# A fused sparse-attention and PReLU-MLP kernel: one token chunk taken off the seven-product scheme, one product split, one sum halved

## Chip, cores and metric

The kernel runs on one core of a Trainium2 chip. The metric is the device time of one execution in microseconds: 337.81 us before the change (median of three runs, 337.74 to 339.4).

## What is computed

Eight batches of eight heads, 576 positions, head size 64. Four heads use a local mask of 32 positions, four a strided mask. The attention output, laid out as 4608 tokens of 512 features, goes through a two-layer network whose activation is a PReLU with one slope per hidden feature:

```python
mask_local = (rel >= 0) & (rel < stride)                       # heads 0 to 3
mask_strided = (rel >= 0) & (pos[None, :] % stride == pos[:, None] % stride)   # heads 4 to 7
attn = softmax(where(mask, q @ k.T / 8, -1e9))
x = (attn @ v).transpose(0, 2, 1, 3).reshape(4608, 512)
h = x @ w_in                                                    # 512 -> 2048
g = np.maximum(h, 0.0) + alpha * np.minimum(h, 0.0)
out = g @ w_out                                                 # 2048 -> 512
```

## The kernel before

The network is done in nine chunks of 512 tokens, numbered 0 to 8. The attention of later batches is cut into small pieces that are laid between the steps of the network, so that TensorE (PE) is kept busy. The order of all instructions on each engine is the order in which the Python code emits them: each engine works off its own list in that order, and waits where an operand or a buffer isn't ready.

A chunk has two parts. **Layer 1** (`lin1_piece`) has 16 pieces. Each makes 128 of the 2048 hidden features for 512 tokens with four matmuls (line 637) into one of three PSUM banks hb0 to hb2, which `hbank` hands out in turn. ScalarE (ACT) takes the negative part (line 647), and VectorE (DVE) finishes the PReLU and writes it as f16 into gT (line 650, the "finish"). Only then is the bank free. The finish is put into the list `late`, which the next attention step empties.

**Layer 2** is done plainly in chunk 0: `lin2_piece`, 16 steps of four 512-column matmuls (line 664), and for each 128 tokens a copy by ACT (line 669) and a store. In chunks 1 to 8 `lin2_sums` computes the same product of a 512 x 2048 and a 2048 x 512 matrix as two by two blocks with seven products in place of eight. Each product has two halves (`mt` 0 and 1) of eight 256-column matmuls (line 759). It needs four sums of blocks of gT, called gsum 0 to 3 in the profile (g1, g2, g4, g3 in the code, line 706), each 128 x 2048 in f16, and four differences of blocks of w_out, made once (`w_sums`, line 694; the third, w3, overwrites a block of w_out). The index p in the code stands for these products:

- p 0 is P1, block (0,0) of gT with block (0,0) of w_out, bank A
- p 1 is P5, gsum 0, bank B; p 2 is P6, gsum 1, added on to bank A
- p 3 is P3, gsum 2, added on to bank B; p 4 is P7, gsum 3, added on to bank A, with w3
- p 5 is P2, block (0,1) of gT, bank C; p 6 is P4, block (1,1) of gT, added on to bank A

ACT copies the banks to SBUF after P1, P5 and P6 (k1, k5, k2, line 771). After P3, P7 and P2, DVE adds a bank and one of these copies into an output tile (line 774), which the sync queue stores. The fourth output tile is a copy by ACT after P4. Chunks 7 and 8 ("quiet", no attention is left) run the products in the order of p. Chunks 1 to 6 run P1, P2, P5, P6, P3, P7, P4.

Who makes the sums: in chunk 1 all four are on DVE, the one for P7 as two halves between layer-1 pieces (after pieces 10 and 12). In chunks 2 to 6 these two halves are on GpSimd (POOL), and the other three on DVE: two at the start of layer 2, the third at its step 4.

Attention works on pairs of heads, four pairs per batch. For batches 2 and up: `transpose_piece` turns q and k of the local heads with PE (line 252) into a PSUM tile from a pool of three banks ("ps"), and DVE copies q, ACT copies k to SBUF (lines 194 and 192); `tails` does the last 64 positions (line 282, the "tail transpose"). q and k of the strided heads are loaded by POOL's queue into qsd and ksd and turned by a transposing DMA on the sync queue (line 141). `score_both` makes scores (line 412), ACT takes the exponential (lines 425 and 431), POOL multiplies by the mask (lines 427 and 434). `pv_piece` multiplies by v (line 455), into the same three banks, and DVE divides by the row sum (lines 462 and 464). POOL also converts and rearranges loaded q, k and v (line 196) and issues many loads.

Of the kernel before, what the change touches and what calls it, by code (L numbers as in the profile page):

```python
# [9 lines left out]
F32 = mybir.dt.float32  # L10
# [21 lines left out]
def kernel(  # L32
# [10 lines left out]
    nc = tc.nc  # L43
    keep = tc.keep_in_program_order

    B, H, S, D = q.shape
# [8 lines left out]
    spool = ctx.enter_context(tc.tile_pool(name="stage", bufs=3))  # L55
# [5 lines left out]
    kpool = ctx.enter_context(tc.tile_pool(name="kp", bufs=1))  # L61
# [26 lines left out]
    turn, busy = [0, 1], []  # L88
# [101 lines left out]
    def cast_copy(eng, o, i):  # L190
        if eng == "act":
            keep(nc.scalar.copy(o, i))
        elif eng == "dve":
            keep(nc.vector.tensor_copy(o, i))  # L194
        else:
            keep(nc.gpsimd.tensor_copy(o, i))
# [41 lines left out]
    def transpose_piece(u, nm):  # L238

        b, strided = u // 2, u % 2 == 1
        early = b < NEARLY
        src = cast16[(b, strided, nm)]
        dst = qTs[u % 2][:, :, 0:576] if nm == "q" else kTs[u % 2][:, :, 32:608]
        tp = pspool.tile([128, 8, 64, 2], F16, tag="ps", name="tp")
        for j in range(8):
            blk = (src[:, j % 2, 128 * (j // 2) : 128 * (j // 2) + 128] if strided  # L250
                   else src[:, j].rearrange("p f d -> p (f d)"))
            keep(nc.tensor.transpose(tp[:, j].rearrange("r p e -> r (p e)"), blk, ident))  # L252
        if strided:
            main = tp.rearrange("r j p e -> r e j p")
            o = dst.rearrange("r e (j p) -> r e j p", j=8)[:, :, :, 0:64]
        else:
            main = tp.rearrange("r t p e -> r e p t")
            o = dst[:, :, 0:512].rearrange("r e (p t) -> r e p t", t=8)
        if early:
            for e in range(2):  # L260
                eng = "dve" if (nm == "q") == (e == 0) else "act"
                if u == 0 and nm == "q":
                    eng = "act"
                if nm == "k" and e == 1:
                    tails(b, u, strided)
# [277 lines left out]
    for g in range(7, npair + 2):  # L543
        c = g // 4
# [68 lines left out]
    late = []  # L613
# [82 lines left out]
    def g_sum(eng, n, which, k0, k1):  # L696

        g = gTs[n]
        g1, g2, g4, g3 = gsum
        o, x, y, op = {  # L700
            1: (g1, quad(g, 1, 0), quad(g, 1, 1), ALU.add),
            2: (g2, g1, quad(g, 0, 0), ALU.subtract),
            3: (g3, quad(g, 0, 0), quad(g, 1, 0), ALU.subtract),
            4: (g4, quad(g, 0, 1), g2, ALU.subtract),
        }[which]
        keep(eng.tensor_tensor(o[:, k0:k1], x[:, k0:k1], y[:, k0:k1], op=op))  # L706
# [10 lines left out]
    def quiet(n):  # L717

        return n >= NCH - 2

    def lin2_sums(n, i):

        g = gTs[n]
        last = n == NCH - 1
        p, mt = i // 2, i % 2
        if i == 0:
            tiles = [banks[z] for z in turn]
            lay.clear()
# [27 lines left out]
        dst = lay[bank][mt]  # L756
        own = mt == 0 or (last and bank == "A")
        for kf in range(8):
            keep(nc.tensor.matmul(  # L759
                dst, lhs[:, kf, 128 * mt : 128 * mt + 128], rhs[:, kf, :],  # L760
                start=(first and own and kf == 0), stop=(kf == 7), skip_group_check=True))

        def each(fn, o, *more):

            if last and bank == "A":
                fn(o[:, mt], lay["A"][mt], *[z[:, mt] for z in more])
            elif mt == 1:
                fn(o, lay[bank + "f"].rearrange("p (m c) -> p m c", m=2), *more)

        def act(o, x):  # L770
            keep(nc.scalar.copy(o, x))  # L771

        def add(o, x, y):
            keep(nc.vector.tensor_tensor(o, x, y, op=ALU.add))  # L774

        def new(nm):
            if mt == 0:
                pool, tag = (kpool, nm) if nm[0] == "k" else (opool, "osb")
                if nm == "k1":
                    pool, tag = (spool, "v") if quiet(n) else (kpool, "k2")  # L780
                held[nm] = pool.tile([128, 2, 256], F32, tag=tag, name=nm, **({"bufs": 2} if tag == "v" else {}))
            return held[nm]

        if p == 0:
            each(act, new("k1"))
        elif p == 1:
            each(act, new("k5"))
        elif p == 2:
            each(act, new("k2"))
        elif p == 3:  # L790
            each(add, new("o12"), held["k2"])
            if mt:
                store(n, 0, 1, held["o12"])
        elif p == 4:
            each(add, new("o22"), held["k5"])
            if mt:
                store(n, 1, 1, held["o22"])
        elif p == 5:
            each(add, new("o11"), held["k1"])
            if mt:  # L800
                store(n, 0, 0, held["o11"])
# [130 lines left out]
    for n in range(1, NCH):  # L932
        ab = attn_until(n + 1) if n + 1 < B else len(pieces)
        left = ab - pos["i"]
        skip = 4 if n == 1 else 0
        acc = 0.0
        for i in range(30):
            if i < 16:
                if quiet(n):
                    lin1_piece(n, 8 * (i % 2) + i // 2)  # L940
                    if i in (3, 7, 11):
                        late.append(lambda i=i: g_sum(nc.gpsimd, n, 1, i // 2 - 1, i // 2 + 1))
                else:
                    lin1_piece(n, i)
                    if i in (10, 12):
                        g_sum(nc.vector if n == 1 else nc.gpsimd, n, 3, 2 * i - 20, 2 * i - 16)
                if n == 1 and i == 6:
                    w_sums(nc.vector, (3,))
            else:
                lin2_sums(n, i - 16)  # L950
            if i >= skip:
# [38 lines left out]
```

The softmax here doesn't subtract the row's maximum and nothing guards it: scores larger than these inputs give would overflow.

## Time and profile before

The profiled execution took 345.34 us, 343.6 us from the first to the last instruction. That is longer than the timed runs.

| engine | busy us | share of the span | instructions |
|---|---|---|---|
| PE (matmul) | 310.0 | 90% | 2861 |
| DVE | 239.6 | 70% | 412 |
| ACT | 174.7 | 51% | 325 |
| POOL | 174.5 | 51% | 170 |

The chain of work that ended last is PE for 67% of the span, DVE for 18%, and ACT and DMA for 5% each. The chunks start at 33.3 us (chunk 0), 72.4, 120.0, 156.8, 190.2, 224.0, 257.2, 287.9 and 313.9.

How to read the lines that follow: a timeline line has the start, the duration, the engine, the source line, the operation, output<-input with shapes, the count, and in brackets the idle time in front of it and what ended that. A line of the table of waits has who waited for whom, then the total in us, the number of times and the longest. In the table by stretches "x" stands ahead of the number of instructions.

### The profile page before, as it was taken

The numbers are of one execution on the slowest core, as the hardware profiler recorded it, in microseconds if no ns is written. First come the engines' busy times: TensorE is split into PE (matmuls) and PEld (weight loads), VectorE is DVE, ScalarE is ACT, GpSimd is POOL, SyncE is SP. The second block draws the span as 40 slices with busy tenths as digits, with TensorE's granted clock in tenths as the row PEclk, the third lists the DMA queues.
The fourth block names the chain that finished last, engine by engine and source line by source line (L and its number), as shares of the span: only waits on it lengthen the run. The fifth ranks groups of instructions, "written<-read, shape, count | busy, mean of one in ns | idle before, by whom it ended". The sixth has DMA issues, their size and how long they took to land.

```text
span 343.6 us, 7176 instructions
## 1 busy us (share of the span) xinstructions
PE 310.0 (90%) x2861; PEld 203.4 (59%) x2861; DVE 239.6 (70%) x412; ACT 174.7 (51%) x325; POOL 174.5 (51%) x170
## 2 busy tenths in 40 slices
PE   6699999999377979899989998999899999999995
PEld 2355445544146734685477887855774586486484
DVE  4336774669998447965895589568847994874872
ACT  1345655547333556447735763577357615633640
POOL 8762595031946868466938690869071720300300
PEclk9659999999969989999999999999999999999999
DMA  7999999399209699169919990897171013003003
GB/s 228 179 207 208 247 165 153 70 166 264 40 19 124 112 236 139 20 133 258 126 18 138 273 117 23 124 171 91 32 156 50 19 38 106 0 2 123 0 2 122
DMA packets 81569, 40.38 MB, mean 118 GB/s; under 512 B 58480, under 2 KB 77184, under 8 KB 81536
## 3 DMA queue, kind: packets, MB, share of 16 engines
q0 software_dynamic: 41728, 17.38, 44.3%
q1 hardware_dynamic: 39808, 22.55, 28.4%
q8 instruction: 22, 0.36, 0.4%
q14 instruction: 11, 0.09, 0.1%
HBM read 38.01 MB, written 9.44 MB: 138 GB/s over the span
## 4 chain that ended last, share of the span: by engine, by line
PE 67%; DVE 18%; ACT 5%; DMA 5%; issue 2%; SPq 0%; ACTq 0%; DVEq 0%
PE hb L637 27%; PE hb L759 23%; DVE gsum L706 6%; DVE gT L650 5%; PE hb L664 4%; DMA kT<-ksd 3%; DMA kl<-in_k_dram 2%; PE pv L455 2%; PE hb L826 2%; DVE x L464 2%; DVE o L774 2%; PE tp L252 2%; ACT neg L647 2%; DVE qT L194 1%; PE sp L412 1%
## 5 line engine op out<-in xcount | busy, mean ns | idle before, releaser
L637 PE MATMUL hb<-xT,win 128*128 128x512 f16 (+1 forms) x640 | 135.4, 362 | 6.0 <-DVE gT L650 5.3
L650 DVE SCALAR_TENSOR_TENSOR gT<-neg,oma,hb 128x512 f16<-128x512 f32 x144 | 105.3, 743 | 43.8 <-ACT neg L647 36.9
L647 ACT ACTIVATE neg<-hb 128x512 f32<-128x512 f32 x144 | 86.0, 597 | 50.0 <-PE hb L637 49.7
L637 PEld LDWEIGHTS <-win 128*128 128x128 f16 x640 | 60.8, 98 | 63.5 <-issue 11.0
L427 POOL TENSOR_TENSOR et<-et,consts 128x576 f16<-128x576 f16 (+1 forms) x24 | 30.6, 1277 | 77.2 <-ACT et L425 77.1
L759 PEld LDWEIGHTS <-gsum 128*128 128x128 f16 x512 | 47.3, 98 | 6.7 <-DVE gsum L706 0.8
L706 POOL TENSOR_TENSOR gsum<-gT 128x1024 f16<-128x1024 f16 (+1 forms) x16 | 28.0, 1765 | 43.0 <-DVE gT L650 43.0
L759 PEld LDWEIGHTS <-gT 128*128 128x128 f16 x384 | 36.1, 98 | 9.5 <-issue 4.1
L464 DVE TENSOR_TENSOR x<-pv,rc 96x384 f16<-96x384 f32 (+2 forms) x62 | 33.0, 532 | 2.1
L434 POOL TENSOR_TENSOR et<-et,consts 128x576 f16<-128x576 f16 (+1 forms) x24 | 32.4, 1349 | 1.8 <-ACT et L431 0.9
L759 PE MATMUL hb<-wout,gT 128*128 128x256 f16 x248 | 31.8, 275 | 0.0
L462 DVE RECIPROCAL rc<-pv 72x6 f32<-72x6 f32 (+2 forms) x80 | 14.7, 183 | 24.1 <-PE pv L455 24.0
L455 PEld LDWEIGHTS <-et 72*128 72x128 f16 (+1 forms) x448 | 24.6, 99 | 11.5 <-POOL et L434 3.1
L759 PE MATMUL hb<-wsum,gsum 128*128 128x256 f16 x248 | 31.0, 273 | 0.0
L759 PE MATMUL hb<-wout,gsum 128*128 128x256 f16 x248 | 30.2, 273 | 0.7 <-DVE gsum L706 0.7
L771 ACT COPY k<-hb 128x512 f32<-128x512 f32 (+1 forms) x24 | 13.6, 568 | 31.7 <-PE hb L759 31.7
L774 DVE TENSOR_TENSOR o<-hb,k 128x512 f32<-128x512 f32 (+1 forms) x24 | 16.3, 680 | 16.9 <-PE hb L759 12.7
L425 ACT ACTIVATE et<-sp 128x576 f16<-128x576 f32 (+1 forms) x24 | 15.5, 647 | 15.0 <-PE sp L412 15.0
L706 DVE TENSOR_TENSOR gsum<-gT 128x2048 f16<-128x2048 f16 (+2 forms) x12 | 21.9, 1824 | 0.3
L826 PE MATMUL hb<-gsum 128*128 128x512 f16 x44 | 18.1, 486 | 1.2 <-DVE gsum L838 1.2
L431 ACT ACTIVATE et<-sph 128x288 f16<-128x288 f32 (+1 forms) x48 | 18.1, 410 | 1.9 <-PE sph L412 1.9
L184 POOL DMA_DIRECT2D vl<-in_v_dram x8 | 11.2, 1403 | 14.4 <-PE pv L455 13.3
(108 smaller groups left out, 340.2 us busy)
## 6 DMA issues: line engine op xcount, KB each, us to landing
out_dram<-o SPq DMA_DIRECT2D x31, 256.0 KB, 2.9
ql<-in_q_dram SPq DMA_DIRECT2D x6, 512.0 KB, 5.4
kl<-in_k_dram SPq DMA_DIRECT2D x6, 512.0 KB, 7.3
stv<-in_v_dram POOLq DMA_DIRECT2D x8, 288.0 KB, 7.4
vl<-in_v_dram POOLq DMA_DIRECT2D x6, 384.0 KB, 9.0
win<-in_moe_w_in_dram POOLq DMA_DIRECT2D x4, 512.0 KB, 9.1
wout<-in_moe_w_out_dram POOLq DMA_DIRECT2D x4, 512.0 KB, 13.5
qsd<-in_q_dram POOLq DMA_DIRECT2D x6, 288.0 KB, 7.1
```

Source lines behind the costliest of these rows:

```text
L427: keep(nc.gpsimd.tensor_tensor(mv, mv, m, op=ALU.mult))
L431: keep(nc.scalar.activation(ev[:, n * y : n * y + n], sps[y][0:r, 0:n], AF.Exp, scale=SCALE))
L434: keep(nc.gpsimd.tensor_tensor(mv, mv, m, op=ALU.mult))
L455: keep(nc.tensor.matmul(pv[:, 65 * x : 65 * x + 65], et[0:r, c : c + 128], v16[0:r, 2 * P.pr + hh, t, :] if P.strided else v16[:, 6 * (2 * ...
L464: keep(nc.vector.tensor_tensor(P.x16[0:w, c0 : c0 + 64 * nb].rearrange("r (c e) -> r c e", e=64), pvv[:, :, 0:64], rc[0:w, 0:nb].unsqueeze ...
L637: keep(nc.tensor.matmul(hps[:, dst : dst + w], win16[:, kk, 128 * m : 128 * m + 128], xT[:, kk, src : src + w], start=(kk == 0 and x == 0) ...
L647: keep(nc.scalar.activation(neg, hps, AF.Relu, scale=-1.0))
L650: keep(nc.vector.scalar_tensor_tensor(gTs[n][:, m, :], neg, oma[:, m : m + 1], hps, op0=ALU.mult, op1=ALU.add))
L706: keep(eng.tensor_tensor(o[:, k0:k1], x[:, k0:k1], y[:, k0:k1], op=op))
L759: keep(nc.tensor.matmul(dst, lhs[:, kf, 128 * mt : 128 * mt + 128], rhs[:, kf, :], start=(first and own and kf == 0), stop=(kf == 7), skip ...
L774: keep(nc.vector.tensor_tensor(o, x, y, op=ALU.add))
L826: keep(nc.tensor.matmul(wps, wrm[:, 0:128], wrm, start=True, stop=True))
```

## The change

It has five parts. Chunk 1 gets the plain layer 2 of chunk 0, so it needs no sums; w3 is therefore made in chunk 2, and the attention pieces are spread over 32 steps there. In chunks 2 to 6 the first half of P2 stays after P1, and its second half moves behind P7; the order is P1, P2 first half, P5, P6, P3, P7, P2 second half, P4, and the next chunk takes the banks in the order B, C, A. The first sum is made in two halves, the first of them after layer-1 piece 13. ACT copies the transposed q as well as k. The copies of P1, P5 and P6 go straight into the output tiles, into which DVE then adds, so the tiles for partial results are gone and the pool of output tiles has four in place of three. The split is meant to put work between P7 and P4, the halving to have the first sum ready sooner, and the rest to take work off DVE.

```diff
-    opool = ctx.enter_context(tc.tile_pool(name="op", bufs=3))
+    opool = ctx.enter_context(tc.tile_pool(name="op", bufs=4))
...
-        cast_copy("dve" if nm == "q" else "act", o, main)
+        cast_copy("act", o, main)
...
-            turn[:] = [turn[1], turn[2], turn[0]] if quiet(n) else [turn[2], turn[1], turn[0]]
+            turn[:] = [turn[1], turn[2], turn[0]]
...
             else:
-                g_sum(nc.vector, n, 1, 0, 8)
+                g_sum(nc.vector, n, 1, 4, 8)
                 g_sum(nc.vector, n, 2, 0, 8)
-        if i == (1 if quiet(n) else 4):
+        if i == (1 if quiet(n) else 3):
             g_sum(nc.vector, n, 4, 0, 8)
...
-        p = (p if quiet(n) else (0, 5, 1, 2, 3, 4, 6)[p])
+        if not quiet(n) and 2 <= i < 12:
+            p, mt = ((5, 0), (1, 0), (1, 1), (2, 0), (2, 1), (3, 0), (3, 1), (4, 0), (4, 1), (5, 1))[i - 2]
...
         if p == 0:
-            each(act, new("k1"))
+            each(act, new("o11"))
         elif p == 1:
-            each(act, new("k5"))
+            each(act, new("o22"))
         elif p == 2:
-            each(act, new("k2"))
-        elif p == 3:
-            each(add, new("o12"), held["k2"])
+            each(act, new("o12"))
+        elif p in (3, 4, 5):
+            r, c = ((0, 1), (1, 1), (0, 0))[p - 3]
+            o = held[f"o{r + 1}{c + 1}"]
+            each(add, o, o)
             if mt:
-                store(n, 0, 1, held["o12"])
+                store(n, r, c, o)
...
-        for i in range(30):
+        for i in range(32 if n == 1 else 30):
...
-                    if i in (10, 12):
-                        g_sum(nc.vector if n == 1 else nc.gpsimd, n, 3, 2 * i - 20, 2 * i - 16)
-                if n == 1 and i == 6:
+                    if n > 1 and i in (10, 12):
+                        g_sum(nc.gpsimd, n, 3, 2 * i - 20, 2 * i - 16)
+                    if n > 1 and i == 13:
+                        late.append(lambda: g_sum(nc.vector, n, 1, 0, 4))
+            elif n == 1:
+                lin2_piece(n, i - 16)
+            else:
+                lin2_sums(n, i - 16)
+                if n == 2 and i == 20:
                     w_sums(nc.vector, (3,))
-            else:
-                lin2_sums(n, i - 16)
             if i >= skip:
-                acc += left / ((19 if n == B - 2 else 20.5) - 0.5 * skip) * (0.5 if i < 16 else 1.0)
+                acc += left / ((22.5 if n == 1 else 19 if n == B - 2 else 20.5) - 0.5 * skip) * (0.5 if i < 16 else 1.0)
             cnt = int(acc)
-            if i == 27 and cnt == 0 and pos["i"] < ab:
-                cnt = 1
```

More of the change, by code (lines that the diff above doesn't have):

```diff
@@ L60 @@
     gpool = ctx.enter_context(tc.tile_pool(name="gp", bufs=1))
-    kpool = ctx.enter_context(tc.tile_pool(name="kp", bufs=1))
     npool = ctx.enter_context(tc.tile_pool(name="np", bufs=3))
-    opool = ctx.enter_context(tc.tile_pool(name="op", bufs=3))
+    opool = ctx.enter_context(tc.tile_pool(name="op", bufs=4))
     pspool = ctx.enter_context(tc.tile_pool(name="ps", bufs=3, space=bass.MemoryType.PSUM))
@@ L777, in new @@
             if mt == 0:
[L778 to L781, printed above, removed]
+                held[nm] = opool.tile([128, 2, 256], F32, tag="osb", name=nm)
             return held[nm]
         if p == 0:
-            each(act, new("k1"))
+            each(act, new("o11"))
         elif p == 1:
-            each(act, new("k5"))
+            each(act, new("o22"))
         elif p == 2:
-            each(act, new("k2"))
-        elif p == 3:
-            each(add, new("o12"), held["k2"])
-            if mt:
-                store(n, 0, 1, held["o12"])
[L794 to L801, printed above, removed]
+            each(act, new("o12"))
[3 more added lines that the diff above has]
+            each(add, o, o)
+            if mt:
+                store(n, r, c, o)
         else:
@@ L944 @@
                     lin1_piece(n, i)
-                    if i in (10, 12):
-                        g_sum(nc.vector if n == 1 else nc.gpsimd, n, 3, 2 * i - 20, 2 * i - 16)
-                if n == 1 and i == 6:
-                    w_sums(nc.vector, (3,))
+                    if n > 1 and i in (10, 12):
[4 more added lines that the diff above has]
+                lin2_piece(n, i - 16)
             else:
                 lin2_sums(n, i - 16)
+                if n == 2 and i == 20:
+                    w_sums(nc.vector, (3,))
             if i >= skip:
-                acc += left / ((19 if n == B - 2 else 20.5) - 0.5 * skip) * (0.5 if i < 16 else 1.0)
+                acc += left / ((22.5 if n == 1 else 19 if n == B - 2 else 20.5) - 0.5 * skip) * (0.5 if i < 16 else 1.0)
             cnt = int(acc)
-            if i == 27 and cnt == 0 and pos["i"] < ab:
-                cnt = 1
             acc -= cnt
```

## The prediction

> **What bounds the kernel now.** I read the table by stretches first, cut at the chunk borders (each starts with the first layer-1 matmul, line 637), then the table of waits, then the timelines of VectorE (DVE), GpSimd (POOL) and TensorE (PE) inside the worst stretch, and last the sync queue's timeline.
>
> The table by stretches, for chunk 1, chunk 2, chunk 3 and chunk 7 (columns: stretch and length, busy us of PE, weight loads, DVE, ACT, POOL, granted clock, DMA share, GB/s):
>
> ```profile
> 72.40:120.00 47.60, 35.99 (x363) 23.43 (x362) 38.79 (x51) 23.02 (x44) 25.54 (x25) 0.93 0.72 124
> 120.00:156.80 36.80, 33.15 (x316) 21.56 (x315) 24.63 (x44) 19.66 (x36) 24.59 (x22) 0.95 0.98 134
> 156.80:190.20 33.40, 31.58 (x318) 21.29 (x317) 24.62 (x44) 19.44 (x37) 23.23 (x21) 1.00 0.89 133
> 287.90:314.00 26.10, 26.10 (x177) 17.14 (x176) 18.02 (x24) 11.90 (x21) 3.46 (x3) 1.00 0.10 33
> ```
>
> PE is the bound everywhere, but chunk 1 takes 14.2 us more than chunk 3 for similar work. Its PE is idle 47.60 - 35.99 = 11.6 us. DVE is busy 38.8 us there against 24.6. Timelines of chunk 1, DVE:
>
> ```profile
> 84.36 1.75 DVE L706 TENSOR_TENSOR gsum<-gT 128x1024 f16<-128x1024 f16 x1
> 87.35 7.65 DVE L706 TENSOR_TENSOR gsum<-gT 128x1024 f16<-128x1024 f16 x1
> 99.71 2.15 DVE L706 TENSOR_TENSOR gsum<-gT 128x2048 f16<-128x2048 f16 x1
> 101.89 2.17 DVE L706 TENSOR_TENSOR gsum<-gsum,gT 128x2048 f16<-128x2048 f16 x1
> ```
>
> POOL and PE over the same time:
>
> ```profile
> 85.51 2.47 POOL L196 COPY vs<-stv 72x1024 f16<-72x1024 f16 x2
> 87.93 0.81 POOL L176 DMA_DIRECT2D stv<-in_v_dram  x1
> 90.00 1.27 POOL L434 TENSOR_TENSOR et<-et,consts 128x576 f16<-128x576 f16 x1
> 93.42 1.03 POOL L196 CAST kl<-kl 128x1024 f16<-128x1024 f32 x1
> ...
> 91.33 0.36 PE L455 MATMUL pv<-vl,et 128*128 128x65 f16 x6 [2.62 <-POOL et L434]
> 96.40 1.86 PE L637 MATMUL hb<-xT,win 128*128 128x512 f16 x4 [4.71 <-DVE gT L650]
> 104.82 0.30 PE L412 MATMUL sph<-qT,kT 64*128 64x72 f16 x7 [2.21 <-DVE x L464]
> ```
>
> A half sum of 1024 columns takes 7.65 us and ends 0.55 us after POOL's unbroken run ends at 94.45; uncontended it takes 0.68 (row "gsum<-gsum,gT 128x1024", 684 ns). Behind it on DVE stand the layer-1 finishes (line 650) that free PE's banks, so PE stops 4.71 us. After the stop the first four matmuls take 1.86 us, not 1.04: the clock has dropped. Elsewhere PE has two small, regular waits:
>
> ```profile
> PE hb L759 <- DVE o L774: 3.5, 6, 0.6
> PE tt L282 <- ACT kT L192: 3.3, 3, 1.1
> PE tt L282 <- DVE qT L194: 2.3, 2, 1.5
> ```
>
> **What the Trainium skill says.** "SBUF — State Buffer", section "SBUF: two separate sides": VectorE and GpSimd share a port pair, an exclusive lock held for a whole instruction, taken by a VectorE operation with two SBUF inputs against a GpSimd operation that reads SBUF; the loser blocks. The trace agrees (7.65 us for 0.68 us of work). The finish (line 650) has one input in PSUM and shows no such block (743 ns in the mean of 144), so only the f16 sums are exposed. "TensorE: Matmul & The Clock Gate", section "What's actually happening": after an idle window of about 3.4 us the clock halves until PE is busy as long again; the 1.86 us above agrees.
>
> **Part by part.**
>
> *Chunk 1 plain.* PE: out go 112 matmuls of 256 columns, in come 64 of 512. Chunk 7 gives both prices: 112 in 12.24 us and 64 (layer 1) in 13.81 us, so +1.57 us, all on the path. DVE loses in chunk 1 five sums (1.75 + 7.65 + 2.15 + 2.17 + 1.21 = 14.9 us as profiled), three adds (2.1) and, with the next edit, two q copies of 1.22; w3 (line 694, 1.22) moves to chunk 2. ACT keeps four output copies of 0.58. With no two-SBUF-input work on DVE, its waits of 4.71, 2.21, 0.78, 0.61 and 0.60 us go. The order of instructions also puts the second mask of pair 8 in front of the first of pair 9 on POOL, and pair 8's second value product one layer-1 piece later: POOL then reaches it at about 88.7 against PE's 88.1, so 2.62 becomes about 0.65. Full-clock work of chunk 1: 13.81 + 12.24 + attention; chunk 3's attention is 31.58 - 26.05 = 5.5, and chunk 1 has one more transposed q/k/tail group (1.0) and two more scores (0.4 each): about 32.9. So slow clock costs 35.99 - 32.9 = 3.1. New length 32.9 + 1.57 + 0.65 + 0.6 for small waits = 35.7: a gain of 11.9 us in the profiled run.
>
> *q copy on ACT.* It takes about 1.0 us (kT's copy of that shape on ACT: 1012 ns) in place of 1.22 on DVE. ACT has idle time right there (1.60 us before k1 in chunk 2). On DVE the copy stood behind two sums; on ACT it follows the transposes at once. The built program gives the tail transpose the bank of the q transposes, so its wait (0.78, 1.1, 1.1, 1.5, 1.1 in chunks 1 to 5; the last four count here) ends: -4.8 us.
>
> *P2 split.* Its second half now stands between P7 (index 4), whose add reads bank A, and P4 (index 6), which writes it. Half a product is 8 x 109 ns = 0.87 us, more than the 0.60 wait that it covers: five chunks (2 to 6), -2.9 us. Price: P5 comes 0.87 us earlier, so g1 must be ready.
>
> *First sum in halves.* The first half now stands in front of the finishes of pieces 14 and 15 on DVE, and in front of the reciprocal and product of a value piece. It meets POOL: in chunk 5 the second mask holds POOL from 239.09 to 240.35, and the half would be issued at about 239.2. I take it that it waits out that one mask (as at 84.36, 99.71 and 101.89) and ends at 241.0 in place of 239.9. Then come the value piece and two finishes at 0.69 us each: finish 15 is at 243.0, not 241.26. P2's first half needs finish 15, and PE is there at 241.97: a new wait of about 1.05 us in chunks 2 to 5, +4.2 us. Chunk 6 has no POOL work at that moment: there g1 and g2 end about as before; its 0.65 wait shrinks to about 0.3. If the lock is missed at the first chance (87.35 did so), another 1.3 us in chunks 2 and 3, where DMA issues follow the mask.
>
> *w3 in chunk 2* lengthens DVE's queue by 1.22 us before a value piece's reciprocal: about +0.3.
>
> *Outputs kept in place.* The adds and copies keep count and size; the four tiles come round once per chunk, long after their store (2.9 us median): zero. Bank order B, C, A leaves 2.6 us between the add on C and its reuse: zero.
>
> *A side effect.* On the sync queue o12's store now stands in front of the q and k transposes for the next chunk (in chunks 2 to 5), and waits for o12's add. By my count k's transpose is issued at 153.0 in chunk 2 in place of 150.7, when the score that needs it comes at 160.1. It landed in 4.3 us there but in 9.3 in chunk 1, where stv's load was issued 0.6 us after it. With the delay it meets stv's load (153.06). Lands at 157.3 (no wait) or 162.3 (2.2 us and a cold clock, as chunk 2 lost 1.84 + 1.8). I take 1 us each in chunks 3 to 5: +3. Chunk 2 keeps its loss.
>
> Sum, profiled: -11.9 - 4.8 - 2.9 - 0.35 + 4.2 + 0.3 + 3 = -12.4.
>
> **From profiled to timed.** The profiled execution took 345.3 us, the timed 337.8: 7.5 us of its waits aren't in the timed runs. If they are all chunk 1's long block (4.71, most of 3.1 of clock), the timed gain is 12.4 - 7.5 = 4.9, so 333; if none is, 325. I take half: 12.4 - 3.75 = 8.7, so 329.
>
> **Rivals.**
> - *Little was blocked in the timed runs* (chance 0.25): then 333, and up to 336 if k's transposes cost another us in each of chunks 3 to 5. For: the 7.5 us gap, and that such a block is a matter of 0.1 us. Against: the other sums of chunk 1 (1.75, 2.15, 2.17) were blocked too.
> - *All was blocked, transposes on time* (0.12): 337.8 - 12.4 - 3 = 322.
> - *Slower* (0.10): the transposes land 9.3 us after issue in chunks 3 to 6 (2.2 + 1.8 each = 16 in place of 3) and the half sum misses the lock twice (+2.6), while the long block wasn't in the timed runs: 333 + 13 + 2.6 = 348; half of that, 341. Against: stv isn't loaded in chunk 5, and chunks 3 to 5 had 10.8 us for the transfer and needed 4.3.
> - *Main case* (0.53): 329.
>
> Range 322 to 336. Faster 0.85 (main, all-blocked, most of the first rival), same 0.06, slower 0.09.
>
> **What would show it.** Right: chunk 1 at about 36 us with no DVE operation over 1.3 us; no wait of the tail transposes or for line 774 in chunks 2 to 6; a new wait of about 1 us ahead of P2's first half, ending with finish 15, and the first half sum at about 1.8 us. Wrong: k's transposes ending PE's waits in chunks 3 to 6, or chunk 1 still above 40 us from POOL's masks.

## The result, and the profile after

The change made the kernel faster: 325.54 us in the median of four executions (324.77 to 326.24), against 338.61 us for the kernel before in the same comparison (337.74 to 339.89). The ratio is 0.9611, with a 95% interval of 0.9566 to 0.9656, or 11.6 to 14.7 us less. The profiled execution took 325.21 us, with a span of 323.4 us. Here and below, medians and ranges count every execution, while the ratios leave out those that are over 1.5% longer than the fastest of their kernel.

The table by stretches of the kernel after, for chunks 1, 2 and 5, cut at the first layer-1 matmul of each chunk:

```profile
68.92:104.59 35.67, 35.03 (x316) 17.85 (x315) 19.70 (x40) 24.49 (x46) 24.43 (x25) 1.00 0.95 165
104.59:137.75 33.16, 31.62 (x315) 21.02 (x314) 25.57 (x45) 20.67 (x37) 23.84 (x22) 1.00 0.93 129
203.96:238.16 34.20, 31.48 (x316) 21.11 (x314) 24.39 (x44) 20.67 (x37) 20.46 (x17) 1.00 0.82 106
```

Chunk 1 fell from 47.6 us to 35.67 us, and PE is idle for 0.64 us of it in place of 11.6. Its clock is 1.00 in place of 0.93, and DVE's busy time is 19.7 us in place of 38.8. Chunk 2 went from 36.8 to 33.2. Chunk 5 went the other way, from 33.23 to 34.20. Chunk by chunk, with the start-up ahead of chunk 0 (all us):

| | start-up | 0 | 1 | 2 | 3 | 4 | 5 | 6 | 7 | 8 and end |
|---|---|---|---|---|---|---|---|---|---|---|
| before | 33.30 | 39.09 | 47.64 | 36.81 | 33.24 | 33.73 | 33.23 | 30.69 | 26.06 | 29.8 |
| after | 29.83 | 39.09 | 35.67 | 33.16 | 32.71 | 33.50 | 34.20 | 29.42 | 26.09 | 29.7 |

The table of waits of the kernel after, its first two lines:

```profile
PE sp L411 <- DMA kT<-ksd: 3.3, 4, 1.7
PE hb L759 <- DVE gT L649: 3.0, 4, 0.8
```

The waits shown of before, of line 759 for an output tile and of the tail transpose for kT and qT, are gone. Two others stand in their place: the first score of chunks 2 to 5 waits for k's transposing DMA, and P2's first half waits for a layer-1 finish. DVE's timeline in chunk 2 of the kernel after shows where the second comes from:

```profile
120.50 1.66 DVE L705 TENSOR_TENSOR gsum<-gT 128x1024 f16<-128x1024 f16 x1
...
122.77 1.39 DVE L649 SCALAR_TENSOR_TENSOR gT<-neg,oma,hb 128x512 f16<-128x512 f32 x2
124.20 0.69 DVE L705 TENSOR_TENSOR gsum<-gT 128x1024 f16<-128x1024 f16 x1
```

The same stretch on POOL:

```profile
120.34 1.26 POOL L433 TENSOR_TENSOR et<-et,consts 72x576 f16<-72x576 f16 x1
```

And two moments on PE, in chunks 2 and 5:

```profile
124.22 1.03 PE L759 MATMUL hb<-wout,gT 128*128 128x256 f16 x8 [0.76 <-DVE gT L649]
...
210.34 0.30 PE L411 MATMUL sp<-qT,kT 64*128 64x72 f16 x8 [1.72 <-DMA kT<-ksd]
```

The first half sum was issued at 120.50, in the middle of a mask that ends at about 121.6, and ended at 122.16. So it took 1.66 us; the second half, with no mask beside it, took 0.69. The value piece and the two finishes follow it, the last finish ends at 124.16, and PE's P2 starts at 124.22 after 0.76 us of waiting. The value product of chunk 1 that had waited 2.62 us for a mask waits 0.39 (at 85.40).

### The profile page after: what moved, and what is told of

Its sections match the earlier page's. It is cut to its first block, busy times and chain, and to the rows that moved or that the text cites. A ratio compares the mean times of both kernels' runs of the same rounds, so it can differ in the third digit from the quotient of the medians.

```text
span 323.4 us, 7079 instructions
## 1 busy us (share of the span) xinstructions
PE 305.6 (94%) x2813; PEld 195.7 (60%) x2813; DVE 220.7 (68%) x403; ACT 180.7 (56%) x331; POOL 172.5 (53%) x170
## 4 chain that ended last, share of the span: by engine, by line
PE 63%; DMA 12%; DVE 12%; ACT 6%; issue 3%; POOL 2%; SPq 1%; ACTq 0%
PE hb L636 22%; PE hb L759 21%; DMA kT<-ksd 10%; PE hb L663 7%; DVE gT L649 6%; PE pv L454 3%; DMA kl<-in_k_dram 2%; DVE gsum L705 2%; DVE x L463 2%; PE hb L817 2%; ACT neg L646 2%; PE sp L411 2%; PE tp L251 1%; PE opl L759 1%; ACT et L430 1%
## 5 line engine op out<-in xcount | busy, mean ns | idle before, releaser
L649 DVE SCALAR_TENSOR_TENSOR gT<-neg,oma,hb 128x512 f16<-128x512 f32 x144 | 105.3, 744 | 43.2 <-ACT neg L646 36.2
L636 PE MATMUL hb<-xT,win 128*128 128x512 f16 (+1 forms) x640 | 132.6, 358 | 0.7
L426 POOL TENSOR_TENSOR et<-et,consts 128x576 f16<-128x576 f16 (+1 forms) x24 | 30.6, 1273 | 64.2 <-ACT et L424 63.8
L759 PEld LDWEIGHTS <-gsum 128*128 128x128 f16 x448 | 41.8, 98 | 5.0
L759 PEld LDWEIGHTS <-gT 128*128 128x128 f16 x336 | 31.4, 98 | 8.3 <-issue 3.4
L461 DVE RECIPROCAL rc<-pv 72x6 f32<-72x6 f32 (+2 forms) x80 | 14.7, 183 | 29.0 <-PE pv L454 28.7
L663 PE MATMUL hb<-wout,gT 128*128 128x512 f16 x128 | 32.7, 379 | 0.1
L433 POOL TENSOR_TENSOR et<-et,consts 128x576 f16<-128x576 f16 (+1 forms) x24 | 30.9, 1287 | 0.9 <-ACT et L430 0.6
L759 PE MATMUL hb<-wout,gT 128*128 128x256 f16 x216 | 27.4, 273 | 3.0 <-DVE gT L649 3.0
L771 ACT COPY o<-hb 128x512 f32<-128x512 f32 (+1 forms) x28 | 15.8, 564 | 24.5 <-PE hb L759 24.2
L759 PE MATMUL hb<-wsum,gsum 128*128 128x256 f16 x216 | 26.2, 273 | 0.0
L759 PE MATMUL hb<-wout,gsum 128*128 128x256 f16 x216 | 26.2, 272 | 0.0
L774 DVE TENSOR_TENSOR o<-hb,o 128x512 f32<-128x512 f32 (+1 forms) x21 | 14.2, 678 | 12.7 <-PE hb L759 8.5
```

What stands on the lines that cost most here:

```text
L426: keep(nc.gpsimd.tensor_tensor(mv, mv, m, op=ALU.mult))
L433: keep(nc.gpsimd.tensor_tensor(mv, mv, m, op=ALU.mult))
L636: keep(nc.tensor.matmul(hps[:, dst : dst + w], win16[:, kk, 128 * m : 128 * m + 128], xT[:, kk, src : src + w], start=(kk == 0 and x == 0) ...
L649: keep(nc.vector.scalar_tensor_tensor(gTs[n][:, m, :], neg, oma[:, m : m + 1], hps, op0=ALU.mult, op1=ALU.add))
L663: keep(nc.tensor.matmul(ops, gTs[n][:, kf, 128 * mt : 128 * mt + 128], wout16[:, kf, :], start=(kf == 0), stop=(kf == 15)))
L759: keep(nc.tensor.matmul(dst, lhs[:, kf, 128 * mt : 128 * mt + 128], rhs[:, kf, :], start=(first and own and kf == 0), stop=(kf == 7), skip ...
```

## The experiments

Chunk lengths are compared from the profiled executions, from chunk 0's start on. The start-up is compared by itself, because it changes from execution to execution without an edit, as the first experiment shows. The experiments ran in four groups, each with the kernel before beside it. Its median was 339.89 us in the group of the first experiment, 336.67 us in that of chunk 1 alone, all but chunk 1, POOL's sums and the first sum whole, 339.99 us in that of the masks, the late store and the last run, and 337.97 us in the remaining one. So results of different groups are compared by their ratios.

### The kernel before, once more

No edit. The question is whether the long half sum of chunk 1 was an accident of one profiled execution, and where the 7.5 us between that execution and the timed ones came from.

> The kernel before, with no edit, profiled a second time. Theory (the 7.5 us by which the profiled execution of before exceeded the timed median are chance losses outside chunk 1: a long start-up of 33.3 us and a wait of chunk 2 for k's transpose): chunk 1 again 47 to 49 us with a half sum of about 7.65 us, chunk 2 at 33 to 35 in place of 36.8, start-up anywhere between 26.5 and 33, and the execution at 335 to 340. Rival (half or all of the 7.5 us was the long block of chunk 1, which timed executions mostly lack): chunk 1 at 40 to 44 us and the half sum under 3 us, in an execution at 336 to 340. Time against before: same.

Measured: 338.43 us (334.37 to 343.25), ratio 1.0027 (0.998 to 1.0074). The profiled execution took 343.25 us, not 335 to 340, and was the longest of the twenty. DVE's second half sum in chunk 1:

```profile
85.98 7.66 DVE L706 TENSOR_TENSOR gsum<-gT 128x1024 f16<-128x1024 f16 x1
```

This duration, and those of the first half sum and of the two whole sums of layer 2's start (1.74, 2.15 and 2.18 us), recur to within 0.01 us, so they belong to the order of the instructions; chunk 1 took 48.7 us. But this execution was a long one too, so alone it does not show that the shorter ones have the block; the next two experiments bear on that.

The theory's second half held only in part: chunk 2 took 35.1 us, 1.8 less than the first time, but its wait for k's transpose came back (1.76 us, against 1.84). What differed was the clock behind it. The same twelve matmuls, first in the first profiled execution, where they follow the stop of 1.84 us:

```profile
126.89 4.45 PE L637 MATMUL hb<-xT,win 128*128 128x512 f16 x12
```

and in this one, behind the stop of 1.76 us:

```profile
126.48 2.77 PE L637 MATMUL hb<-xT,win 128*128 128x512 f16 x12
```

In the first the granted clock was 0.50 for about 3.4 us from 127.0 on, in the second 1.00. In chunk 1 it was the other way round: behind the stop of 2.21 us the clock stayed at 1.00 in the first execution, and behind that of 2.35 us it was 0.50 for about 3.4 us in this one. So the same code, with nearly the same stop, sometimes pays for a stretch of half clock behind it, some 1.7 us, and sometimes does not. The start-up differs by more. The table by stretches for the start-up, first in this execution:

```profile
0.00:31.93 31.93, 26.86 (x239) 14.31 (x240) 15.34 (x48) 12.46 (x25) 20.42 (x35) 0.84 1.21 206
```

and in the first profiled execution of the kernel before:

```profile
0.00:33.30 33.30, 27.20 (x240) 14.73 (x241) 14.97 (x48) 12.55 (x25) 21.04 (x35) 0.80 1.27 205
```

and in the next experiment, whose start-up has the same code:

```profile
0.00:26.52 26.52, 22.73 (x239) 12.34 (x240) 15.21 (x48) 12.55 (x25) 18.41 (x32) 1.00 1.30 205
```

The same work took from 26.5 us at a granted clock of 1.00 to 33.3 us at 0.80; PE's busy time accounts for 4.5 us of the 6.8. The executions without a trace of their own fit this: of the kernel before, in this comparison, those at a mean granted clock of 0.988 to 0.990 took 333.4 to 336.2 us, and those at 0.970 and below 339.9 to 342.9; the first profiled one was 345.3 at 0.965.

An estimate from these figures: a stretch of 3.4 us at half clock takes 0.005 from the mean clock of some 340 us. By that measure the first profiled execution had about seven such stretches (four in the start-up, two in chunk 1, one in chunk 2), an execution at 0.98 about four, and one at 0.99 two. So most of the 7.5 us go with the clock of an execution, and the largest single place where the profiles show that clock to differ is the start-up. The executions without a trace can't be cut into chunks, so for them this stays an estimate.

### Chunk 1 alone

The kernel before with chunk 1 plain (its spacing of the attention pieces and w3's place included) and nothing else changed.

```diff
-        for i in range(30):
+        for i in range(32 if n == 1 else 30):
...
-                    if i in (10, 12):
-                        g_sum(nc.vector if n == 1 else nc.gpsimd, n, 3, 2 * i - 20, 2 * i - 16)
-                if n == 1 and i == 6:
-                    w_sums(nc.vector, (3,))
+                    if n > 1 and i in (10, 12):
+                        g_sum(nc.gpsimd, n, 3, 2 * i - 20, 2 * i - 16)
+            elif n == 1:
+                lin2_piece(n, i - 16)
             else:
                 lin2_sums(n, i - 16)
+                if n == 2 and i == 20:
+                    w_sums(nc.vector, (3,))
...
```

> The kernel before with one part of the change only: chunk 1 takes the plain layer 2 (with w3 made in chunk 2 and the attention spread over 32 steps of chunk 1). Theory: chunk 1's loss is VectorE's two-input f16 sums standing against GpSimd, in the timed runs too; this part alone brings some 9 of the 13 us: 329 to 330 us, with chunk 1 at about 36.5 us in the profile. Rival (the long block is an accident of the profiled execution): 3 to 4 us, so about 335.

Measured: 325.25 us against 336.67, ratio 0.970 (0.9666 to 0.9735), so 9 to 11 us less. The table by stretches, chunk 1:

```profile
66.99:102.80 35.81, 35.03 (x316) 17.82 (x315) 21.78 (x42) 22.73 (x44) 24.59 (x25) 1.00 0.97 165
```

The profiled chunk is 11.8 us shorter, and most of that, not all, is in the timed executions. Had these lacked the long block, about 4.5 us would have been left, an estimate: 11.8 less the stop of 4.7 and the 2.6 of slow clock behind it (PE is busy for 35.03 us here, of which the plain layer 2 adds 1.57; the kernel before was busy for 36.03).

The clocks of the timed executions point the same way. Of the 80 executions of the kernel before whose clock was recorded, none was granted more than 0.990; with chunk 1 plain, two of six were granted 1.00 and the others 0.995. That is what two stretches of half clock in chunk 1 of every execution would give.

### Everything but chunk 1

The kernel after with the seven products in chunk 1 again, as before; the first sum stays whole there.

```diff
-                g_sum(nc.vector, n, 1, 4, 8)
+                g_sum(nc.vector, n, 1, 0 if n == 1 else 4, 8)
...
-        for i in range(32 if n == 1 else 30):
+        for i in range(30):
...
-                    if n > 1 and i in (10, 12):
-                        g_sum(nc.gpsimd, n, 3, 2 * i - 20, 2 * i - 16)
+                    if i in (10, 12):
+                        g_sum(nc.vector if n == 1 else nc.gpsimd, n, 3, 2 * i - 20, 2 * i - 16)
+                    if n == 1 and i == 6:
+                        w_sums(nc.vector, (3,))
...
-            elif n == 1:
-                lin2_piece(n, i - 16)
             else:
                 lin2_sums(n, i - 16)
-                if n == 2 and i == 20:
-                    w_sums(nc.vector, (3,))
...
```

> The changed kernel with chunk 1 back on seven products (its four sums on VectorE, w3 in its layer 1), all other parts kept. Theory: 334 to 335 us, as only the q copy, the split of P2 and the halved sum are left to gain (5.5 and 3.5 us of waits removed, 3.0 put in, transposes' waits 3.3 put in, about 3 to 4 net), and the block of 4 us or more is back in chunk 1. Rival (the rest of the change brought most): 329 to 330.

Measured: 330.75 us, ratio 0.9873 (0.9833 to 0.9913), so 2.9 to 5.6 us less than the kernel before beside it. The time missed the 334 to 335 that were expected, but the kernel before was faster here too (336.67 us); the gain of about 4.3 us is a little more than the 3 to 4 expected. DVE's second half sum in chunk 1:

```profile
80.22 7.66 DVE L705 TENSOR_TENSOR gsum<-gT 128x1024 f16<-128x1024 f16 x1
```

and what PE waited for:

```profile
PE hb L636 <- DVE gT L649: 4.7, 1, 4.7
```

The block of 7.66 us and the stop of 4.7 us are both here, in a profiled execution of 330.12 us, while the others took 330.1 to 331.6 and once 337.7. Here the profiled execution is no longer than the timed ones, with the whole block in it. By the ratios the two parts give 3.0% and 1.3%, together 4.3%, and the whole change 3.9%, within the intervals.

### Are those two half sums the cause?

In the kernel before, the two half sums of chunk 1 go to POOL, as in the later chunks.

```diff
-                        g_sum(nc.vector if n == 1 else nc.gpsimd, n, 3, 2 * i - 20, 2 * i - 16)
+                        g_sum(nc.gpsimd, n, 3, 2 * i - 20, 2 * i - 16)
```

> The kernel before with one edit: in chunk 1 the two half sums for P7 are on GpSimd, as in chunks 2 to 6. Theory (it is these sums, waiting for the port pair in front of the layer-1 finishes, that stop TensorE): the stops of 4.7 us go, but 4.2 us of sums stand in GpSimd's queue in front of masks, which TensorE waits for: net 2 to 5 us faster, 334 to 337, with no VectorE operation over 2.3 us in chunk 1. Rival (chunk 1 loses by all its VectorE load): no change, 338 to 339.

Measured: 338.96 us, ratio 1.0082 (1.004 to 1.0123), a miss: 2 to 5 us less had been expected. Chunk 1 took 49.0 us. DVE, the first sum of layer 2:

```profile
94.96 5.11 DVE L706 TENSOR_TENSOR gsum<-gT 128x2048 f16<-128x2048 f16 x1
```

POOL at that time:

```profile
94.27 1.26 POOL L434 TENSOR_TENSOR et<-et,consts 128x576 f16<-128x576 f16 x1
95.49 1.03 POOL L196 CAST kl<-kl 128x1024 f16<-128x1024 f32 x1
96.48 1.26 POOL L427 TENSOR_TENSOR et<-et,consts 72x576 f16<-72x576 f16 x1
97.72 1.26 POOL L434 TENSOR_TENSOR et<-et,consts 72x576 f16<-72x576 f16 x1
```

The block moved to the next sum. Issued at 94.96, it ended at 100.07, 1.1 us after POOL's unbroken run ended at 98.98, and it needs 1.23. The added POOL sums also pushed the masks back (one value product waited 4.4 us for its mask). So it isn't a matter of the two half sums alone: a whole sum that meets a long run of POOL work is held as well, and moving work to POOL makes the run longer.

### Is it POOL's masks that hold them?

The kernel before without POOL's multiplications by the mask in batch 2, whose attention lies in chunk 1; that batch's mask is left out of the computation.

```diff
-                keep(nc.gpsimd.tensor_tensor(mv, mv, m, op=ALU.mult))
+                if P.b != 2:
+                    keep(nc.gpsimd.tensor_tensor(mv, mv, m, op=ALU.mult))
...
-                if y:
+                if y and P.b != 2:
```

> The kernel before without GpSimd's multiplication by the mask for batch 2 (pairs 8 to 11), so the mask is left out of that batch's attention; nothing else is changed. A part of the GpSimd work beside chunk 1's sums goes, the copies, casts and DMA issues stay. Theory (the sums wait for GpSimd's two-input operations and its copies): the half sum that took 7.65 us takes under 3, the two whole ones 1.2 in place of 2.15, and the stop of 4.7 us goes; about 9 us faster than before. Rival (the sums are slow for another reason, such as their own operands): 7.6 and 2.15 us again, with only TensorE's 2.6 us wait for a mask gone.

Measured: 330.59 us in two executions, ratio 0.9753 (0.9669 to 0.9836). Chunk 1, and two of DVE's sums in it:

```profile
71.20:109.10 37.90, 34.25 (x363) 23.00 (x362) 28.95 (x51) 23.02 (x44) 14.52 (x17) 1.00 0.95 156
...
85.94 0.68 DVE L707 TENSOR_TENSOR gsum<-gT 128x1024 f16<-128x1024 f16 x1
90.67 1.23 DVE L707 TENSOR_TENSOR gsum<-gT 128x2048 f16<-128x2048 f16 x1
```

With the other three (0.69, 1.22 and 1.21 us) the sums take 5.0 us together, against 14.9 in the kernel before (1.75 + 7.65 + 2.15 + 2.17 + 1.21), with no DVE instruction changed. Chunk 1 took 37.9 us, the stop of 4.7 us is gone, and the clock stays at 1.00. So the sums themselves were cheap enough for chunk 1, and what POOL does beside them accounts for 9.7 of the 11.97 us by which the change shortened chunk 1. Not all of the 9.7 goes through the sums: the value product's own wait of 2.62 us for a mask is gone as well.

### The changed kernel again, and with q's copy on DVE

The changed kernel was run again as it is, for the comparisons of this group:

> The changed kernel itself once more, on the chip of the three runs beside it, so that they can be compared with it: 324 to 327 us. Its part from the first layer-1 matmul of chunk 0 to the end should take 293 to 294 us in the profile; what lies ahead of that, unchanged by the edit, may differ by some us.

Measured: 327.32 us (324.11 to 329.43), ratio 0.9679 (0.9614 to 0.9744), so 8.6 to 13.0 us less than the kernel before. From chunk 0 on, the profiled execution took 295.3 us, over the 293 to 294 expected. Chunk 5 has the difference:

```profile
205.95:242.37 36.42, 33.13 (x316) 21.51 (x314) 24.39 (x44) 20.70 (x37) 20.51 (x17) 0.95 0.68 100
...
212.90 0.30 PE L411 MATMUL sp<-qT,kT 64*128 64x72 f16 x8 [2.29 <-DMA kT<-ksd]
```

The stop for k's transpose was 2.29 us here, and a stretch of half clock followed it; in the first profile of this kernel it was 1.72 us, with no such stretch. Chunks 3 and 4, on the other hand, had no stop for k and took 32.6 us each.

Then q's copy was put back on DVE:

```diff
-        cast_copy("act", o, main)
+        cast_copy("dve" if nm == "q" else "act", o, main)
```

> The changed kernel with the copy of the transposed q back on VectorE. Theory: behind two sums there, it holds the bank of the tail transpose again: waits of 1.1 to 1.5 us in chunks 2 to 5, so 4 to 5.5 us slower than the changed kernel, 329 to 331. Rival (the wait for finish 15 now covers it): within 1 us of the changed kernel.

Measured: 330.52 us, ratio 0.9754 (0.9676 to 0.9831). The first line of its table of waits:

```profile
PE tt L281 <- ACT kT L191: 4.4, 4, 1.1
```

The tail transpose waits again in four chunks, 4.4 us together; chunks 2 to 4 took 34.3 to 34.6 us, against 32.6 to 33.6 in both profiles of the changed kernel. The medians differ by 3.2 us in that direction; the two intervals overlap, so the wait is shown and the gain in time only likely.

### P2 unsplit

The changed kernel with both halves of P2 behind P1.

```diff
-            p, mt = ((5, 0), (1, 0), (1, 1), (2, 0), (2, 1), (3, 0), (3, 1), (4, 0), (4, 1), (5, 1))[i - 2]
+            p, mt = ((5, 0), (5, 1), (1, 0), (1, 1), (2, 0), (2, 1), (3, 0), (3, 1), (4, 0), (4, 1))[i - 2]
```

> The changed kernel with both halves of P2 behind P1 again. Theory: P4's wait for the add after P7 is back (0.6 us in five chunks, 2.9), but o12's store falls behind the transposes of q and k again, so their wait (3.3) goes: within 1.5 us of the changed kernel. Rival (the split is a gain in itself, and the order on the sync queue costs nothing): 3 us slower, 328 to 329.

Measured: 327.84 us, ratio 0.9699 (0.9636 to 0.9762), the same as the changed kernel beside it. From its table of waits:

```profile
PE hb L759 <- DVE o L774: 2.9, 5, 0.6
```

Unsplit, the wait of 0.6 us comes back in five chunks, and the wait for k's transposes shrinks to one of 1.0 us. The split earns its 2.9 us and hands about as much back on the sync queue, as the next experiment shows more directly.

### The store of o12 behind the transposes

The changed kernel with o12's store held back until o22's.

```diff
-            if mt:
-                store(n, r, c, o)
+            if mt and (quiet(n) or p == 5):
+                store(n, r, c, o)
+            elif mt and p == 4:
+                store(n, 0, 1, held["o12"])
+                store(n, r, c, o)
```

> The changed kernel with o12's store held back until o22's, so that it stands behind the transposes of q and k in chunks 2 to 6; the first sum stays in halves. Theory: the waits for k's transposes in chunks 3 to 5 go (2.9 us in the first profile of the changed kernel), the finish waits stay: 2 to 3 us faster than the changed kernel, and k's transposes land in 4 to 5.5 us. Rival (the delay comes from stv's load alone): no change.

Measured: 324.58 us, ratio 0.9546 (0.9477 to 0.9616). The wait for k's transposes is down to one of 0.8 us, in chunk 2. Chunks 3, 4 and 5 took 32.55, 32.58 and 32.51 us, against 32.71, 33.50 and 34.20 in the kernel after: 0.2 + 0.9 + 1.7 = 2.8 us was the price of the side effect there. In the second profile of the changed kernel (32.57, 32.60 and 36.42) it was 3.9 us, all of it in chunk 5.

### The first sum whole

The changed kernel with the first sum in one piece at the start of layer 2.

```diff
-                g_sum(nc.vector, n, 1, 4, 8)
+                g_sum(nc.vector, n, 1, 0, 8)
...
-                    if n > 1 and i == 13:
-                        late.append(lambda: g_sum(nc.vector, n, 1, 0, 4))
```

> The changed kernel with the first sum whole again, after finish 15. Theory: the wait of P2's first half for finish 15 (4 times 0.75 us) goes and no wait of P5 for the sum comes, since the sum (1.23 us) ends before TensorE is there: 3 us faster than the changed kernel, 322 to 323. Rival (the halving was needed for P5, which comes 0.87 us earlier now): P5 waits instead, 325 to 326.

Measured: 321.53 us, ratio 0.9568 (0.9517 to 0.9619). DVE in chunk 2, at the place shown of the kernel after:

```profile
117.73 1.39 DVE L649 SCALAR_TENSOR_TENSOR gT<-neg,oma,hb 128x512 f16<-128x512 f32 x2
119.16 1.23 DVE L705 TENSOR_TENSOR gsum<-gT 128x2048 f16<-128x2048 f16 x1
```

The finishes come first, and the whole sum takes 1.23 us after them, with no mask beside it. The wait for finish 15 is gone, and in chunks 2 to 5 no wait of P5 for the sum has come. One of 0.38 us for a sum is left, in chunk 6, where the kernel before had 0.65 and the kernel after none. So the halving bought PE nothing in chunks 2 to 5, and about half a microsecond in chunk 6 (29.96 us whole, 29.42 halved).

### Both mends together

The first sum whole and o12's store late:

> The changed kernel with the first sum whole (after finish 15) and o12's store held back until o22's, so that it stands behind the transposes of q and k. Theory: both waits that the change put in go: 3.0 for finish 15 and 2.9 of 3.3 for the transposes (chunk 2's 0.5 comes from chunk 1's store and stays), so some 6 us faster than the changed kernel, 319 to 320. Rival (the transposes are late because they share the DMA engines with stv's load): 322 to 323, as with the whole sum alone.

Measured: 318.53 us, ratio 0.9451 (0.9389 to 0.9514). The sync queue before the end of chunk 4, in this kernel:

```profile
189.76 1.20 SPq L486 DMA_TRANSPOSE xs<-x16s  x1
191.07 1.34 SPq L140 DMA_TRANSPOSE qT<-qsd  x1
192.50 1.96 SPq L140 DMA_TRANSPOSE kT<-ksd  x1
194.55 5.43 SPq L712 DMA_DIRECT2D out_dram<-o  x4
```

and in the kernel after:

```profile
195.08 1.20 SPq L486 DMA_TRANSPOSE xs<-x16s  x1
199.23 0.38 SPq L712 DMA_DIRECT2D out_dram<-o  x1
199.71 1.32 SPq L140 DMA_TRANSPOSE qT<-qsd  x1
201.11 2.28 SPq L140 DMA_TRANSPOSE kT<-ksd  x1
```

In the kernel after, the queue stands idle from 196.28 to 199.23, because its next entry is the store of o12, and that waits for o12's add on DVE (198.51 to 199.20). The transposes stand behind it. Chunk 5 starts at 203.96, so k's transpose was issued only 2.9 us ahead of it, and the score that needs it ran at 210.34. Here the four stores come after both transposes, and k's is issued 6.3 us ahead of chunk 5 (198.80). Chunks 2 to 5 took 32.46, 31.68, 31.62 and 31.52 us, 3.8 less than with the late store alone (33.46, 32.55, 32.58, 32.51), while chunk 6 took 29.96 in place of 29.43. So halving costs 3.3 us net.

Last, the same with chunk 1's third output store also held behind the transposes there:

```diff
-            keep(nc.sync.dma_start(out[r0 : r0 + 128, :], osb))
+            if n == 1 and mt == 2:
+                ops_cur["held"] = (r0, osb)
+            else:
+                keep(nc.sync.dma_start(out[r0 : r0 + 128, :], osb))
...
+        elif part == 0 and n == 1 and mt == 3:
+            r1, held3 = ops_cur.pop("held")
+            keep(nc.sync.dma_start(out[r1 : r1 + 128, :], held3))
```

> The changed kernel with the first sum whole, o12's store held back, and chunk 1's third store held back by a layer-2 step, so that it too stands behind the transposes. Theory: the last wait for k's transposes (0.8 us in chunk 2) goes: 0 to 1 us faster than with o12's store alone held back. Rival: k's transposes are late there for sharing the DMA engines with stv's load, and the wait stays.

Measured: 318.09 us, ratio 0.9422 (0.9351 to 0.9492). No wait for k's transposes is left; against the run before it, the time is the same within the intervals. These two beat both kernels, at about 5.5% to 5.8% under the kernel before.

## Why the prediction was right, and where its steps failed

The prediction was 329 us in a range of 322 to 336, and faster; the kernel took 325.5. The mechanism was right: chunk 1's sums stood against POOL, and without them the chunk lost what was forecast. The step from the profiled to the timed gain failed, and the chunk terms agree with the result in part by luck.

- **Chunk 1, -11.9 us, new length 35.7.** Measured 35.67, with every wait named there gone and the clock at 1.00. The length fits more closely than its terms. By its own terms the full-clock work is 31.58 + 1.0 + 2 x 0.4 = 33.4, not 32.9, so the sum should have read 36.2. PE's busy time bears out 33.4 (33.4 + 1.57 = 35.0; measured 35.03), and so the slow clock cost 2.6 us, not 3.1. The waits left over came to 0.64 us in place of 1.25. The two errors cancel. Without POOL's masks the chunk loses 9.7 us too, so the named cause is shown, not only the gain.
- **"I take half" of 7.5 us as chunk 1's block.** This step failed. It took 3.75 us off the gain for a block that timed executions were taken to lack in part. But the half sum takes 7.65 or 7.66 us in each of three profiles of that order, one of them of an execution as short as its neighbours, and the clocks of 80 executions leave room for its slow stretches in all of them. Chunk 1 alone brought 9 to 11 us, where 11.9 less 3.75 would be 8.2. By the estimate above, most of the 7.5 us go with the granted clock, which was 0.80 in that execution's start-up, at a cost of up to 6.8 us, and 0.95 in its chunk 2, 1.7 us. The prediction looked for the gap in the worst chunk and did not look at the start-up's clock. A reproducible wait was taken for noise because the noise had not been located. It does not follow that a profiled gain is found whole in the timed runs: from chunk 0 on, the two profiles of before are 14.3 to 16.7 us longer than the two of after, while the timed gains were 13.1 us (11.6 to 14.7) and, in the second comparison, about 10.8 (8.6 to 13.0), which the forecast 8.7 just reaches. Where the rest lies isn't settled. That the sum of the parts, 12.4, comes near 13.1 is in part luck, since chunk 2 gained more than its terms said.
- **"Chunk 2 keeps its loss."** Wrong, in the kernel's favour. In both profiles of before, chunk 2 waited 1.8 us for k's transpose; after, and with chunk 1 alone changed, 0.5 us, and 0.9 in the second profile of after. In before, the load of stv was issued on POOL's queue 0.6 us after that transpose (117.76 against 117.17), and the score ran 9.4 us after the issue; after, stv's load was ahead of it (101.95 against 102.42) and the score ran 7.3 us after. The order is what the trace shows; that it is the cause wasn't tried. What is left of the wait went when chunk 1's third store was held back. Chunk 2 was to shrink by 0.35 us and shrank by 1.9 against the second profile of before (3.65 against the first, of which 1.7 is the slow clock).
- **q's copy, -4.8 us.** Those waits are gone, and 4.4 us come back with the copy on DVE. Right in mechanism; the timed difference of 3.2 us is within the spread.
- **P2 split, -2.9 us.** The wait of 0.6 us in chunks 2 to 6 is gone, and it is back unsplit: 2.9 us in five.
- **First sum in halves, +4.2 us.** The half sum was put at about 1.8 us and took 1.66, waiting out one mask, and PE's wait was put at 1.05 us in each of chunks 2 to 5 and was 3.0 in four. By chunk lengths the halving costs 3.8 us there, and chunk 6 gains 0.5 where 0.35 was given. The rival's second missed chance of the lock did not happen.
- **k's transposes, +3 us.** The issue in chunk 2 was put at 153.0 in the time of before, 3.8 us ahead of the chunk's end, and came at 134.93, 2.8 us ahead. PE waited for k in chunks 3, 4 and 5 for 0.19, 0.94 and 1.72 us, and by chunk lengths the price is 2.8 us, or 3.9 in the second profile, so the size was right and the even spread of 1 us each was not. Such waits were also named as a sign of the forecast being wrong, although the sum had priced them.
- **w3, outputs kept in place: +0.3 and zero.** With chunk 1 alone changed, w3 lengthens DVE's busy time in chunk 2 by 1.1 us (25.75 against 24.63), and no wait of PE names it. Nothing speaks against zero for the outputs on PE; one add on DVE waited 0.65 us for a store of its tile, which the text had ruled out, and nothing waited for that add.

Of the rivals, "little was blocked in the timed runs" falls with chunk 1 alone, which gained 9 to 11 us where about 4.5 would have been left, and with the short profiled execution that has the block. "All was blocked, transposes on time" had the first half right and the second wrong: the transposes were late, and with them mended the time went to 324.6, and with the halving undone as well to 318.5. The slower case needed stops of 2.2 us with a cold clock in each of four chunks; that came once in the two profiles, in chunk 5 of the second (2.29 us, clock 0.95).

The Trainium skill, "SBUF — State Buffer", section "SBUF: two separate sides", says that VectorE and GpSimd exclude each other on a shared port pair for a whole instruction. The experiment without masks agrees (0.68 us in place of 7.65). The runs add that the sum may go on waiting while POOL starts one instruction after the other: at 94.96 in the kernel with POOL's sums it was let in only after three further POOL instructions had begun and ended, and at 120.50 in the kernel after at the first boundary. What decides between the two stays open; no run here tells it.

The prediction puts the halving of the clock down to an idle window of about 3.4 us. Here the measurement decides: the half clock lasted about 3.4 us each time, but it also came behind stops of 1.84, 2.29 and 2.35 us, and did not come behind others of 1.72, 1.76 and 2.21 us. So a stop of about 2 us may cost 1.7 us more than its length.

## What to carry to other kernels

Before a gap between a profiled and a timed execution is taken off a gain, find where it lies: compare two profiles of the same kernel stretch by stretch, the granted clock included; a wait that recurs to a hundredth of a microsecond belongs to the code, while the slow clock behind it may not recur. A sum moved to an earlier place on an in-order queue delays what stands behind it, so look for what the next engine waits for there, not only at the sum. When matmuls are reordered, the stores and transposes on the queue that issues them are reordered too, and may give the gain back, as here 2.9 us against 2.8 in one profile and 3.9 in the other.

## What the runs showed that was not expected

- A two-input f16 sum of 0.68 us on DVE can be held for 7.65 us while POOL works without a gap, the same to 0.01 us in three profiles; moving the sums to POOL moved the block to a 2048-column sum, which took 5.11 us in place of 1.23.
- The exclusion works both ways: in the kernel before, a mask beside the sum at 101.89 took POOL 2.25 us in place of 1.26.
- The start-up, with unchanged code, took 26.5 to 33.3 us, with granted clocks of 1.00 to 0.80.
- One store in front of a transposing DMA on the sync queue stopped PE for up to 2.29 us, though its own issue took 0.4 us: the queue had stood idle for it (2.95 us in the place shown), until the tile to be stored was ready.
